# Wider input transfers for two batches, a last key chunk of 128, and a residual turned by DMA in an attention and wave-MLP kernel

## The chip, the cores and the metric

The kernel runs on one NeuronCore of one Trainium2 chip. The core has five engines that run side by side, each in its own order: TensorE (PE, matmuls; its weight loads are listed as PEld), VectorE (DVE), ScalarE (ACT), GpSimd (POOL) and SyncE (SP, which here only issues DMAs). Inputs and outputs lie in HBM; the engines work on SBUF, and matmuls write PSUM. The metric is device time in microseconds (us), less is better. The time before is 260.9 us, the median of 11 runs (260.03 to 262.04).

## What is computed

Two stages, cut from the reference to what matters:

```python
# q, k, v: (8 batches, 8 heads, 576 positions, 64)
q_d, k_d, v_d = mean over 4 neighbouring positions          # 144 positions
out_up    = repeat(softmax(q_d k_d^T / 8) v_d, 4)           # pooled attention
out_local = softmax(where(|i - j| < 4, q k^T / 8, -1e9)) v  # banded attention
x = (out_up + out_local) as (8, 576, 512)                   # heads side by side
theta = x @ w_theta
y = w_tok_r @ (x * cos(theta)) + w_tok_i @ (x * sin(theta)) # over positions
u = x + y
out = u + relu(u @ w_ch)                                    # float32
```

## The kernel before

**Stages.** For each batch, steps named by one letter each are done: L loads q, k, v into float32 staging tiles (`st`, eight buffers); C casts them to bf16 (`q_tm`, `k_tm`, `v_w`); A turns q and k so that head dimensions lie on partitions (`qT`, `kT`, pairs of heads stacked on 128 partitions) and makes the pooled `qdT`, `kdP` and `vd`; S makes scores and their exponentials (`pd` pooled, `pm` banded, five chunks of keys) and masks the band; N makes the pooled output (`xd`, `xdT`), V the banded output (`tmp`), T turns it and adds both (`xT`); H makes theta and cosine and sine (`cs`), M and Z the products (`z`, nine blocks of 128 rows: real and imaginary for 576 positions); X mixes over positions with the turned weights (`psu` from `WT` and `z`, eight products of nine matmuls of 288 columns a batch) and adds `xT` (`uT`); U turns `uT` by a transposing DMA into `utm`; R multiplies by `w_ch` (`psr`); O adds the residual and stores. Lower-case l and c load and cast the weights, W turns the token weights (nine `WT` blocks), and D is a warm-up of six matmuls of 512 columns that computes nothing.

**Order.** The steps of all kinds are laid out by hand as strings of letters: `FIRST`, then `PERIOD` three times, then `LAST`. A letter means the next step of its kind. After each step `pin()` ties every instruction to the one before it on its engine, so the strings are the order on each engine and on SP's queue of DMA issues. All input DMAs and all but one store are issued by SP.

**Chunks.** Queries are cut at 0, 120, 240, 360, 480 (`QS`); the keys that a chunk of queries can see start at `KS` and are `KW` long: four chunks of 128 and a last one from 476 of 100. For the pooled v, 120 positions of each chunk are summed by the matrices `PU` (one for the first chunk, one for the others). The mask of a chunk is a pair of affine selects on POOL (lines 442 and 444), for batch 0 a product with a `band` matrix on DVE (line 435).

**Batches 0 and 1** (`WIDE`) load q and k in another form than the rest (line 92): partition p holds positions 6p to 6p+5 of a head, so 96 partitions are used and a contiguous run is 6 x 64 floats, 1.5 KB; a transfer holds heads 2hh and 2hh+1, and there are four for q and four for k. `wide_turn` (from line 299) then turns one pair of heads with six matmuls of 96 columns, copies the result (q on ACT, k on DVE, line 309) and sums groups of four on DVE (lines 316, 319, 322). Later batches load positions onto partitions with runs of one head, 256 B. Casts of batch 0 are split: q on DVE, k on ACT, v on POOL; all later ones are POOL's.

**Residual.** For batches in `DMA_U` (1 to 6) the residual of the first 512 positions is `utm`, turned by DMA (line 621, one issue for each of four blocks of 128 channels), and DVE does relu and sum in one instruction (line 673). For batches 0 and 7 PE turns it into PSUM (`psx`, line 642), ACT applies relu (line 662) and DVE adds (line 678). The last 64 positions are always done in the second way.

Of the kernel before, what the change touches and what calls it, by code (L numbers as in the profile page):

```python
# [15 lines left out]
P = 128  # L16
# [12 lines left out]
QC = [120, 120, 120, 120, 96]  # L29
KS = [0, 116, 236, 356, 476]  # L30
KW = [128, 128, 128, 128, 100]
QN = [128, 128, 128, 128, 96]
# [3 lines left out]
TR = 96  # L36
NTR = 6
TP = TR // 4
TW = TR + TP

# [7 lines left out]
def kernel(  # L48
# [34 lines left out]
    def stage(b, key):  # L83
        t = staged[b, key] = stg.tile([P, 1024], FP32, tag="st", name=f"st{b}_{key}")
        return t

    def load(b):

        if b < WIDE:
            for hh in range(4):  # L90
                for nm, src in zip("qk", (q, k)):
                    nc.sync.dma_start(
                        out=stage(b, f"{nm}{hh}")[0:TR, 0:2 * NTR * D].rearrange("p (h e) -> p h e", h=2),
                        in_=src[b, 2 * hh:2 * hh + 2].rearrange("h (p r) d -> p h (r d)", r=NTR),
                    )
                    yield
        else:
            for nm, src in zip("qk", (q, k)):
                for i in range(3):
                    t = stage(b, f"{nm}{i}")[0:TR].rearrange("p (c h d) -> p c h d", c=2, d=D)  # L100
                    for j in range(2):
                        c = 2 * i + j
                        nc.sync.dma_start(
                            out=t[:, j], in_=src[b, :, TR * c:TR * c + TR, :].rearrange("h p d -> p h d"),
                        )
                    yield
        for i in range(3):
            t = stage(b, f"v{i}").rearrange("p (c h d) -> p c h d", c=2, d=D)
            for c in range(2 * i, min(2 * i + 2, NCH)):
                nc.sync.dma_start(  # L110
                    out=t[0:KW[c], c % 2],
                    in_=v[b, :, KS[c]:KS[c] + KW[c], :].rearrange("h p d -> p h d"),
                )
            yield

    def cast(b):

        q_tm = work.tile([TR, NTR, H, D], BF16, tag="q_tm", bufs=1, name=f"q_tm{b}")
        k_tm = work.tile([TR, NTR, H, D], BF16, tag="k_tm", bufs=1, name=f"k_tm{b}")
        v_w = v_ws[b % 2]  # L120
        inputs[b] = (q_tm, k_tm, v_w)
        eng = CASTS.get(b, CASTS[None])
        if b < WIDE:
            for hh in range(4):
                for i, dst in enumerate((q_tm, k_tm)):
                    eng[i](out=dst[:, :, 2 * hh:2 * hh + 2, :].rearrange("p r h d -> p h r d"),
                           in_=staged.pop((b, f"{'qk'[i]}{hh}"))[0:TR, 0:2 * NTR * D].rearrange(
                               "p (h r d) -> p h r d", h=2, d=D))
                    yield
        else:  # L130
            for i, dst in enumerate((q_tm, k_tm)):
                for c in range(3):
                    eng[i](out=dst[:, 2 * c:2 * c + 2].rearrange("p c h d -> p (c h d)"),  # L133
                           in_=staged.pop((b, f"{'qk'[i]}{c}"))[0:TR])
                    yield
        for i in range(3):
            t = staged.pop((b, f"v{i}")).rearrange("p (c h d) -> p c h d", c=2, d=D)
            n, rows = (2, P) if i < 2 else (1, KW[4])
            eng[2](out=v_w[0:rows, 2 * i:2 * i + n, :, 0:D], in_=t[0:rows, 0:n])  # L139
            yield  # L140
# [46 lines left out]
    PU = []  # L187
    for lo in (0, 4):
        r = const.tile([P, KP], BF16, name=f"pu{lo}")
# [15 lines left out]
    band = []  # L205
    for off in (3, -1):
        r = const.tile([P, P], BF16, name=f"band{len(band)}")
# [20 lines left out]
    def weight_loads():  # L228

        def two(w, nm):  # L230
            for i in range(2):
                nc.sync.dma_start(out=stage("w", f"{nm}{i}").rearrange("p (c e) -> p c e", c=2),
                                  in_=w[256 * i:256 * i + 256, :].rearrange("(c p) e -> p c e", p=P))
                yield
# [11 lines left out]
    def weight_casts():  # L246

        for i in range(2):
            act(out=wth[:, 2 * i:2 * i + 2, :].rearrange("p c e -> p (c e)"), in_=staged.pop(("w", f"th{i}")))
            yield  # L250
# [6 lines left out]
        for i in range(2):  # L257
            gp(out=wch[:, 2 * i:2 * i + 2, :].rearrange("p c e -> p (c e)"), in_=staged.pop(("w", f"ch{i}")))
            yield
# [32 lines left out]
    def turns(b):  # L292
# [8 lines left out]
        def wide_turn(n, hh):  # L301
            tm, To = ((q_tm, qT), (k_tm, kT))[n]
            ps = w2(f"pstr{n}{hh}_{b}")
            for r in range(NTR):
                nc.tensor.matmul(
                    out=ps[:, r // 3, (r % 3) * TR:(r % 3) * TR + TR],
                    lhsT=tm[:, r, 2 * hh:2 * hh + 2, :], rhs=ip[:, 0:TR], start=True, stop=True,
                )
            (dve if n == 1 else act)(
                out=To[:, hh, :].rearrange("p (w k c) -> p w k c", k=2, c=3),  # L310
                in_=ps[:, :, 0:3 * TR].rearrange("p k (c w) -> p w k c", w=TR),
            )
# [12 lines left out]
        def turn(n, c):  # L325
            tm, To = ((q_tm, qT), (k_tm, kT))[n]
            ps = w1(f"pstr{n}{c}_{b}")[:, 0:4 * TW].rearrange("p (hh w) -> p hh w", w=TW)
            for hh in range(4):
                nc.tensor.matmul(  # L329
                    out=ps[:, hh, :], lhsT=tm[:, c, 2 * hh:2 * hh + 2, :], rhs=ip, start=True, stop=True,  # L330
                )
# [23 lines left out]
        for c in range(4):  # L355
            nc.tensor.matmul(out=psb[KP * c:KP * c + KP, 0:2 * D], lhsT=PU[1][0:KW[4], :],
                             rhs=v_w[0:KW[4], 4, c::4, 0:D], start=True, stop=True)
# [14 lines left out]
    def scores(b):  # L372
# [28 lines left out]
        for h in range(H):  # L401
            par, r = h % 2, KP * (h % 4)
            nc.tensor.matmul(
                out=ps[r:r + KP, h // 4, SD:2 * SD],
                lhsT=kdP[64 * par:64 * par + 64, h // 2, 4, :],
                rhs=qdT[64 * par:64 * par + 64, h // 2, :],
                start=True, stop=True,
            )
# [7 lines left out]
        for c in range(NCH):  # L416
# [17 lines left out]
            if b in DVE_BANDS and c % DVE_BANDS[b] == 0:  # L434
                nc.vector.tensor_tensor(
                    out=pv, in0=pv,
                    in1=band[min(c, 1)][0:kw, 0:qn].unsqueeze(1).to_broadcast([kw, 8, qn]),
                    op=ALU.mult,
# [13 lines left out]
    def pooled_out(b):  # L452
# [3 lines left out]
        for g in range(2):  # L456
            ps = w2(f"psnd{g}_{b}")
            pv = ps[:, :, 0:260].rearrange("p e (j w) -> p e j w", w=65)[0:QD]
            for h in range(H):
                nc.tensor.matmul(  # L460
                    out=pv[:, h // 4, h % 4, :],
                    lhsT=pd[:, h, QD * g:QD * g + QD], rhs=vd[:, 0, h, 0:65],
                    start=(h % 4 == 0), stop=False,
                )
# [24 lines left out]
    def outputs(b):  # L489

        v_w = inputs.pop(b)[2]
        for c in range(NCH):
# [3 lines left out]
            for par in range(2):  # L496
                for j in range(4):
                    nc.tensor.matmul(  # L498
                        out=pv[0:qn, par, j, :],
                        lhsT=pms[b][c][0:kw, 4 * par + j, 0:qn],  # L500
                        rhs=v_w[0:kw, c, 2 * j + par, 0:65],
                        start=(j == 0), stop=(j == 3),
                    )
            rl = work.tile([P, 2, 4], FP32, tag="rl", name=f"rl{c}_{b}")
            nc.vector.reciprocal(out=rl[0:cnt], in_=pv[0:cnt, :, :, 64])
            tmp = tmps[b, c] = work.tile([P, DM], BF16, tag="tmp", bufs=4, name=f"tmp{c}_{b}")
            nc.vector.tensor_tensor(  # L507
                out=tmp[0:cnt].rearrange("p (j e d) -> p e j d", e=2, j=4),
                in0=pv[0:cnt, :, :, 0:D],
                in1=rl[0:cnt].unsqueeze(3).to_broadcast([cnt, 2, 4, D]),  # L510
                op=ALU.mult,
# [105 lines left out]
    def residuals(b):  # L617

        u = u_tm[b] = moep.tile([P, 4, 4, P], BF16, tag="utm", bufs=1, name=f"utm_{b}")
        for dc in range(4):  # L620
            nc.sync.dma_start_transpose(out=u[:, dc], in_=uTs[b][:, dc, 0:512])
            yield
# [44 lines left out]
    def store(b):  # L667
# [19 lines left out]

    DMA_U = (1, 2, 3, 4, 5, 6)

# [5 lines left out]
    FIRST = (  # L695
        "LLLCCLCALLALLCCALACDLCLADACAlAlCSSSClCSLASlScDVlNCcNAlNlVcSDlLcccWcTCLTcVVLHTAZCLVCHTCWALWWWLLTLLCCA"
        "LCWZWAAHLLAHWHADLWCSLCCCMZCLLZASlZlLCXSXACANSAACXLCSLNAAAXNSSXVAccCAXTCALVAACVLXLSTTSSHLVVXLTLHCTZRO"
        "AHZZCLHVLROHRLLMCOCSZZCNRLROSLNALOA"
    )
    PERIOD = (  # L700
        "XSCSNTXCCAAXCUAAVAXUACVAXAVAAVXTSSTAXSTAUTHXULCNHZNCAHLZCVHHCZROLLSLMSZRLOZRORLOLROL"
    )
    PERIODS = 3
    LAST = (
        "ASXVAAAXAAVXACCNAVXAUTACCCSUTTXTASSCXAHXVZUNHCTHXCAUHZNHZSZLLLRCMOLARORSSCZLRSOOCCNAXAXACAVAAVXXAVTA"
        "XUSSTARVXSOSXASTTHVUXVTHUNHZUZHNZHRMOSSZRORZORVXSONXTVTXXTVHXVXUHTZXTZHZUUHXZHMURROZROOXXRORXOXXXXRO"
        "ROXRORORORO"
    )
# [60 lines left out]
```

## Time and profile before

One execution was recorded by the hardware profiler; it took 259.36 us, of which the profile spans 257.6.

| | us |
|---|---|
| median of 11 runs (lowest, highest) | 260.9 (260.03, 262.04) |
| the profiled execution | 259.36 |
| its span, first to last instruction | 257.6 |
| mix products, line 608, 576 matmuls, busy | 80.0 |
| theta, line 546, 128 matmuls, busy | 32.9 |
| products with w_ch, line 632, 128 matmuls, busy | 32.0 |
| POOL's band selects, lines 442 and 444, busy | 73.5 |
| POOL waiting for DMAs of v, k (both forms) and q | 10.2, 8.3 + 6.4, 2.2 |
| warm-ups, line 282, 30 matmuls, busy | 10.4 |

A page of the profile gives busy time of each engine, the span in 40 slices with tenths of busy time, groups of instructions by line with mean duration and what ended the idle time ahead of them, and the chain of work that ended last. A name such as `k_tm<-st_k` is a tile and what it is made from. Matmul ends are modelled: a busy PE is not PE at its peak.

### The profile page before, as it was taken

How to read it: one execution, taken by the hardware profiler on the slowest of the kernel's cores; microseconds unless marked ns; L12 is line 12 of the kernel's file. 1: busy time of each engine (PE TensorE's matmuls, PEld its weight loads, DVE VectorE, ACT ScalarE, POOL GpSimd, SP SyncE). 2: the span in 40 equal slices, each digit the busy share in tenths (PEclk: the TensorE clock that was granted, in tenths of full speed). 3: DMA queues.
4: the chain of work that ended last, by engine and by line, in shares of the span. 5: the costliest groups of instructions: out<-in, count | busy, mean ns of one | idle time of the engine just before them, and what ended most of it. 6: DMA issues, size and time to landing. Idle time of an engine off the chain costs nothing.

```text
span 257.6 us, 7472 instructions
## 1 busy us (share of the span) xinstructions
PE 239.7 (93%) x2960; PEld 168.3 (65%) x2960; DVE 187.5 (73%) x421; ACT 179.0 (69%) x336; POOL 154.6 (60%) x178
## 2 busy tenths in 40 slices
PE   1868869999999999999999999999999999999993
PEld 1434546678667876587657866686768675776762
DVE  4866869767768777768686868785768588876543
ACT  3449489987988779867895689767885887334022
POOL 4244356599997977596839965898079763600000
PEclk9986999999999999999999999999999999999998
DMA  7999999999998994999689987998399122311324
GB/s 188 249 249 319 274 253 193 217 236 240 206 233 214 243 163 95 202 235 260 84 193 223 280 117 158 198 269 191 74 248 222 34 53 87 100 41 43 149 71 150
DMA packets 120851, 46.73 MB, mean 181 GB/s; under 512 B 110448, under 2 KB 114544, under 8 KB 120816
## 3 DMA queue, kind: packets, MB, share of 16 engines
q1 hardware_dynamic: 120736, 46.18, 81.8%
q8 instruction: 23, 0.38, 0.7%
q14 instruction: 12, 0.10, 0.1%
q10 hardware_dynamic: 80, 0.07, 0.1%
HBM read 33.65 MB, written 9.44 MB: 167 GB/s over the span
## 4 chain that ended last, share of the span: by engine, by line
PE 81%; DMA 7%; ACT 4%; DVE 3%; POOL 2%; issue 1%; SPq 1%; DVEq 0%; POOLq 0%
PE psu L608 27%; PE psr L632 10%; PE psth L546 10%; PE pstr L329 6%; DMA w<-in_moe_w_tok_i_dram 5%; PE psS L421 4%; PE psloc L498 3%; PE xTps L528 3%; PE psxt L581 3%; PE wu L282 2%; DMA st_k<-in_k_dram 2%; PE psnd L460 2%; PE psr L650 2%; PE pstl L557 1%; PE psnd L466 1%; PE pszl L592 1%
## 5 line engine op out<-in xcount | busy, mean ns | idle before, releaser
L608 PE MATMUL psu<-WT,z 128*128 128x288 bf16 x576 | 80.0, 286 | 0.0
L608 PEld LDWEIGHTS <-z 128*128 128x128 bf16 x576 | 53.6, 98 | 15.3 <-issue 0.8
L442 POOL TENSOR_SCALAR_AFFINE_SELECT pm<-pm 128x1024 bf16<-128x1024 bf16 (+1 forms) x35 | 36.7, 1050 | 22.2 <-ACT pm L429 22.1
L612 DVE TENSOR_TENSOR uT<-psu,xT 128x288 bf16<-128x288 f32 x64 | 29.2, 456 | 24.1 <-PE psu L608 23.2
L429 ACT ACTIVATE pm<-psS 128x1024 bf16<-128x1024 f32 (+1 forms) x40 | 38.1, 986 | 10.3 <-PE psS L421 10.1
L444 POOL TENSOR_SCALAR_AFFINE_SELECT pm<-pm 128x1024 bf16<-128x1024 bf16 (+1 forms) x35 | 36.8, 1051 | 2.4
L546 PE MATMUL psth<-wth,xT 128*128 128x512 bf16 x128 | 32.9, 379 | 0.6 <-DVE xT L529 0.6
L632 PE MATMUL psr<-wch,uT 128*128 128x512 bf16 x128 | 32.0, 380 | 0.0
L551 ACT ACTIVATE cs<-psth,pihc 128x512 bf16<-128x512 f32 x32 | 22.1, 689 | 11.6 <-PE psth L546 7.9
L507 DVE TENSOR_TENSOR tmp<-psloc,rl 120x512 bf16<-120x512 f32 (+1 forms) x40 | 27.6, 690 | 1.4
L529 DVE TENSOR_TENSOR xT<-xTps,xdT 128x480 bf16<-128x480 bf16 (+1 forms) x40 | 25.0, 632 | 3.5 <-PE xTps L528 2.9
L139 POOL CAST v_w<-st_v 128x1024 bf16<-128x1024 f32 (+1 forms) x24 | 20.9, 899 | 10.2 <-DMA st_v<-in_v_dram 10.2
L582 DVE TENSOR_TENSOR z<-psxt,cs 128x1024 bf16<-128x1024 bf16 x32 | 21.7, 686 | 4.7 <-PE psxt L581 3.2
L133 POOL CAST k_tm<-st_k 96x1024 bf16<-96x1024 f32 x18 | 18.8, 1047 | 9.3 <-DMA st_k<-in_k_dram 8.3
L332 ACT CAST kT<-pstr 128x384 bf16<-128x384 f32 x36 | 18.0, 502 | 7.0 <-PE pstr L329 6.9
L662 ACT ACTIVATE rel<-psr 128x512 f32<-128x512 f32 (+1 forms) x16 | 7.9, 494 | 18.4 <-PE psr L650 15.0
L133 POOL CAST q_tm<-st_q 96x1024 bf16<-96x1024 f32 x18 | 18.4, 1037 | 2.2 <-DMA st_q<-in_q_dram 2.2
L332 ACT CAST qT<-pstr 128x384 bf16<-128x384 f32 x36 | 16.1, 483 | 4.9 <-PE pstr L329 4.7
L552 ACT ACTIVATE cs<-psth 128x512 bf16<-128x512 f32 x32 | 18.9, 591 | 0.0
L673 DVE SCALAR_TENSOR_TENSOR osb<-psr,utm 128x512 f32<-128x512 f32 x24 | 16.4, 688 | 2.4 <-PE psr L632 2.0
L632 PEld LDWEIGHTS <-uT 128*128 128x128 bf16 x128 | 11.1, 98 | 9.8
L498 PE MATMUL psloc<-v_w,pm 128*128 128x65 bf16 (+1 forms) x320 | 16.9, 196 | 0.1
(107 smaller groups left out, 433.0 us busy)
## 6 DMA issues: line engine op xcount, KB each, us to landing
st_v<-in_v_dram SPq DMA_DIRECT2D x32, 256.0 KB, 5.0
out_dram<-osb SPq DMA_DIRECT2D x32, 256.0 KB, 3.7
st_q<-in_q_dram SPq DMA_DIRECT2D x36, 192.0 KB, 4.7
st_k<-in_k_dram SPq DMA_DIRECT2D x36, 192.0 KB, 4.3
st_q<-in_q_dram SPq DMA_DIRECT2D x8, 288.0 KB, 5.9
st_k<-in_k_dram SPq DMA_DIRECT2D x8, 288.0 KB, 11.6
st_v<-in_v_dram SPq DMA_DIRECT2D x8, 200.0 KB
w<-in_moe_w_tok_r_dram SPq DMA_DIRECT2D x2, 576.0 KB
```

What stands on the lines that cost most here:

```text
L133: eng[i](out=dst[:, 2 * c:2 * c + 2].rearrange("p c h d -> p (c h d)"), in_=staged.pop((b, f"{'qk'[i]}{c}"))[0:TR])
L332: nc.scalar.copy(out=To[:, :, TR * c:TR * c + TR], in_=ps[:, :, 0:TR])
L429: nc.scalar.activation(out=pv, in_=ps[0:kw].rearrange("p e (j w) -> p (e j) w", w=P)[:, :, 0:qn], func=AF.Exp, scale=SCL,)
L442: nc.gpsimd.affine_select(out=pv, in_=pv, compare_op=ALU.is_ge, fill=0.0, base=off, pattern=[[0, 8], [-1, qn]], channel_multiplier=1)
L444: nc.gpsimd.affine_select(out=pv, in_=pv, compare_op=ALU.is_ge, fill=0.0, base=6 - off, pattern=[[0, 8], [1, qn]], channel_multiplier=-1)
L498: nc.tensor.matmul(out=pv[0:qn, par, j, :], lhsT=pms[b][c][0:kw, 4 * par + j, 0:qn], rhs=v_w[0:kw, c, 2 * j + par, 0:65], start=(j == 0), ...
L507: nc.vector.tensor_tensor(out=tmp[0:cnt].rearrange("p (j e d) -> p e j d", e=2, j=4), in0=pv[0:cnt, :, :, 0:D], in1=rl[0:cnt].unsqueeze(3) ...
L529: nc.vector.tensor_tensor(out=xT[:, :, QS[c]:QS[c] + cnt].rearrange("p e (m j) -> p e m j", j=4), in0=ps[:, :, 0:cnt].rearrange("p e (m j) ...
L546: nc.tensor.matmul(out=th, lhsT=xT[:, dc, P * c:P * c + P], rhs=wth[:, dc, :], start=(dc == 0), stop=(dc == 3),)
L608: nc.tensor.matmul(out=ps[:, 0:288], lhsT=z[:, j, P * dc:P * dc + P], rhs=WT[:, j, cols], start=(j == 0), stop=(j == 8),)
L612: nc.vector.tensor_tensor(out=uT[:, dc, cols], in0=ps[:, 0:288], in1=xT[:, dc, cols], op=ALU.add)
L632: nc.tensor.matmul(out=psr, lhsT=uT[:, dc, P * c:P * c + P], rhs=wch[:, dc, :], start=(dc == 0), stop=(dc == 3),)
```

## The change

q and k of batches 0 and 1 are read with nine positions to a partition: 64 partitions hold one head, two neighbouring heads fill 128, and a contiguous run is 9 x 64 floats, 2.3 KB. A staging tile takes two such transfers, heads (4g, 4g+1) and (4g+2, 4g+3), and is cast at once into a layout in which heads h and h+2 lie side by side on a partition. So a pair that is turned together is h and h+2; `place` gives pair and half of a head, and the pooled, banded and output steps ask it. Turning takes nine matmuls of 64 columns. The last key chunk starts at 448 and is 128 long, with a pooling matrix and a band matrix of its own. Batch 7 joins `DMA_U`; its last block of 128 channels is turned by four PE transposes and copied by ACT. All three order strings are new; the number of warm-ups stays five.

```diff
-KS = [0, 116, 236, 356, 476]
-KW = [128, 128, 128, 128, 100]
+KS = [0, 116, 236, 356, 448]
+KW = [128, 128, 128, 128, 128]
...
+WR = 9
+WB = 64
...
-            for hh in range(4):
+            for g in range(2):
                 for nm, src in zip("qk", (q, k)):
-                    nc.sync.dma_start(
-                        out=stage(b, f"{nm}{hh}")[0:TR, 0:2 * NTR * D].rearrange("p (h e) -> p h e", h=2),
-                        in_=src[b, 2 * hh:2 * hh + 2].rearrange("h (p r) d -> p h (r d)", r=NTR),
-                    )
+                    t = stage(b, f"{nm}{g}").rearrange("p (e r d) -> p e (r d)", e=2, d=D)
+                    for e in range(2):
+                        h = 4 * g + 2 * e
+                        nc.sync.dma_start(
+                            out=t[:, e], in_=src[b, h:h + 2].rearrange("h (p r) d -> (h p) (r d)", r=WR),
+                        )
                     yield
...
+    def place(b, h):
+
+        return (2 * (h // 4) + h % 2, h // 2 % 2) if b < WIDE else (h // 2, h % 2)
+
+    def wide(t, g):
+
+        return t.rearrange("p c h d -> p (c h d)")[:, 2 * WR * D * g:2 * WR * D * (g + 1)].rearrange(
+            "p (r e d) -> p r e d", e=2, d=D)
...
-            for hh in range(4):
+            for g in range(2):
                 for i, dst in enumerate((q_tm, k_tm)):
-                    eng[i](out=dst[:, :, 2 * hh:2 * hh + 2, :].rearrange("p r h d -> p h r d"),
-                           in_=staged.pop((b, f"{'qk'[i]}{hh}"))[0:TR, 0:2 * NTR * D].rearrange(
-                               "p (h r d) -> p h r d", h=2, d=D))
+                    eng[i](out=wide(dst, g).rearrange("p r e d -> p e r d"),
+                           in_=staged.pop((b, f"{'qk'[i]}{g}")).rearrange("p (e r d) -> p e r d", e=2, d=D))
                     yield
...
-    for lo in (0, 4):
+    for lo in (0, 4, 32):
...
-    for off in (3, -1):
+    for off in (3, -1, -29):
...
-            for r in range(NTR):
+            flat = ps.rearrange("p k n -> p (k n)")[:, 0:S]
+            for r in range(WR):
                 nc.tensor.matmul(
-                    out=ps[:, r // 3, (r % 3) * TR:(r % 3) * TR + TR],
-                    lhsT=tm[:, r, 2 * hh:2 * hh + 2, :], rhs=ip[:, 0:TR], start=True, stop=True,
+                    out=flat[:, WB * r:WB * r + WB], lhsT=wide(tm, hh // 2)[:, r, :, :],
+                    rhs=ident[:, WB * (hh % 2):WB * (hh % 2) + WB], start=True, stop=True,
                 )
...
-            nc.tensor.matmul(out=psb[KP * c:KP * c + KP, 0:2 * D], lhsT=PU[1][0:KW[4], :],
+            nc.tensor.matmul(out=psb[KP * c:KP * c + KP, 0:2 * D], lhsT=PU[2],
                              rhs=v_w[0:KW[4], 4, c::4, 0:D], start=True, stop=True)
...
-            nc.sync.dma_start_transpose(out=u[:, dc], in_=uTs[b][:, dc, 0:512])
+            if b < B - 1 or dc < 3:
+                nc.sync.dma_start_transpose(out=u[:, dc], in_=uTs[b][:, dc, 0:512])
+            else:
+                ps = w1(f"psut_{b}", BF16)[:, 0:512].rearrange("p (c t) -> p c t", t=P)
+                for c in range(4):
+                    nc.tensor.transpose(out=ps[:, c, :], in_=uTs[b][:, dc, P * c:P * c + P], identity=ident)
+                nc.scalar.copy(out=u[:, dc], in_=ps)
             yield
...
-    DMA_U = (1, 2, 3, 4, 5, 6)
+    DMA_U = (1, 2, 3, 4, 5, 6, 7)
...
     FIRST = (
-        "LLLCCLCALLALLCCALACDLCLADACAlAlCSSSClCSLASlScDVlNCcNAlNlVcSDlLcccWcTCLTcVVLHTAZCLVCHTCWALWWWLLTLLCCA"
-        "LCWZWAAHLLAHWHADLWCSLCCCMZCLLZASlZlLCXSXACANSAACXLCSLNAAAXNSSXVAccCAXTCALVAACVLXLSTTSSHLVVXLTLHCTZRO"
-        "AHZZCLHVLROHRLLMCOCSZZCNRLROSLNALOA"
+        "LCLALLCLAllALCCALAAAclCDASDSCSllSSClllALVSLcDccNcccLCcNDCVLVLNTVWWSWLTCTCWLLLACVWHTTACLACHZHAAHALHAD"
+        "WAASZMCZCLZSCWSLlWNZWNCAAACSXNVAAASXTALSLXVLALAXALTSVLCHCTCVXCCHlcVTAXCTcACHZLHCXHZASLSXLZZRLROCSMLR"
+        "OOLSRZOLCSCLLNROALA"
     )
     PERIOD = (
-        "XSCSNTXCCAAXCUAAVAXUACVAXAVAAVXTSSTAXSTAUTHXULCNHZNCAHLZCVHHCZROLLSLMSZRLOZRORLOLROL"
+        "CCANAXAASCSXCANXVAVAXVUAAXLAVASTXCATSSTUATVUHXXHZTHNCUZHRLCLCOHZSLSLMCZROZLRRLORLLOO"
     )
...
     LAST = (
-        "ASXVAAAXAAVXACCNAVXAUTACCCSUTTXTASSCXAHXVZUNHCTHXCAUHZNHZSZLLLRCMOLARORSSCZLRSOOCCNAXAXACAVAAVXXAVTA"
-        "XUSSTARVXSOSXASTTHVUXVTHUNHZUZHNZHRMOSSZRORZORVXSONXTVTXXTVHXVXUHTZXTZHZUUHXZHMURROZROOXXRORXOXXXXRO"
-        "ROXRORORORO"
+        "LAVCACAASXLAVAXAACVNAUAXSSNLXCVATCSTCAASVCUXAATSNAAXASNAUXSSNTTHVXVUZHTHZHTVLHRAOROMCAROALZHZCZSROVC"
+        "CAXTXSSUTAVXZSSTXHVHNNXZUHVNXHMRZSSOXZZXTVUXTUXRTHOVVXHRROOTXZTROHXZXZHUXXZHMURUUROZROXROOXXROXXUXXX"
+        "UURUORORRRROROOO"
     )
```

## The prediction

> **What bounds the kernel now.** First the page: how full each engine is, and where.
>
> ```profile
> span 257.6 us, 7472 instructions
> ...
> PE 239.7 (93%) x2960; PEld 168.3 (65%) x2960; DVE 187.5 (73%) x421; ACT 179.0 (69%) x336; POOL 154.6 (60%) x178
> ...
> PE   1868869999999999999999999999999999999993
> ...
> DMA  7999999999998994999689987998399122311324
> ```
>
> The span is 40 slices of 6.44 us. TensorE (PE) is full from slice 7 (about 40 us) to the end; only the first 40 us and the last slice have holes. So the order of the later work matters only if it makes a hole, and the time is: when PE becomes full, plus the matmul work left. I count that work in columns of the moving operand. Between the first mix products (psu, dc 0, first half) of batches 1 and 2, which the chain of waits starts at 81.77 and 109.03 us, lie 66,824 columns: 2,451 per us. Before batch 0's first mix product (49.13 us) stand 64,776. In all there are 557,504.
>
> The holes before 40 us are read from two more views. The windows (busy time with count for each engine, granted clock, DMA share, GB/s) show what the queue moves when only one kind of load is in it:
>
> ```profile
> 4.00:11.00 7.00, 4.61 (x30) 2.61 (x31) 5.69 (x18) 3.57 (x5) 3.50 (x12) 1.00 1.09 261
> 11.00:16.00 5.00, 4.36 (x38) 2.38 (x36) 3.42 (x8) 2.01 (x3) 1.04 (x1) 1.00 1.31 215
> 18.00:22.00 4.00, 3.62 (x51) 2.03 (x52) 1.50 (x4) 3.15 (x6) 0.62 (x1) 0.50 1.02 368
> 33.00:37.00 4.00, 1.79 (x24) 1.32 (x25) 2.12 (x4) 3.81 (x5) 2.20 (x3) 1.00 1.09 265
> ```
>
> Rows 1 and 4 are q and k of batches 0 and 1 (96 partitions, runs of 1.5 KB): 261 and 265 GB/s. Row 2 is v (runs of 256 B): 215. Row 3 is mostly theta and the token weights, 128 partitions, runs of 2 to 2.3 KB: 368. The DMA share is full throughout: the queue is the bottleneck of the inputs. The waits between 20 and 50 us (total, times, longest) say who suffers:
>
> ```profile
> POOL k_tm L126 <- DMA st_k<-in_k_dram: 6.4, 4, 5.6
> ...
> PE pstr L305 <- POOL k_tm L126: 2.3, 1, 2.3
> POOL v_w L139 <- DMA st_v<-in_v_dram: 2.3, 3, 1.0
> POOL q_tm L133 <- DMA st_q<-in_q_dram: 2.2, 2, 1.1
> ...
> ACT wtm L253 <- DMA w<-in_moe_w_tok_i_dram: 1.8, 2, 1.0
> ```
>
> Batch 1's k, the token weights, then batch 2's q arrive late. VectorE (DVE) bounds only batch 0's turns: busy from 4.67 to 18.24 us with some 2 us of gaps.
>
> **The change, part by part.**
>
> *Transfers of q, k.* 2 x 2.36 MB. At 263 GB/s 18.0 us, at the nearest row (368, same run length and partitions) 12.8: 2.6 us less queue per batch. The Trainium skill (SBUF — State Buffer, "Door 1: The DMA port swizzle") says that the rate follows the ports reached, and its table puts partitions 0-63 on the 8 even ports; so 96 partitions send two thirds of their bytes through half of the ports, and 128 should give 4/3 of 263, 350, an estimate: 2.25 us per batch. I take the row; below, nothing is gained if run length and partitions don't matter. SP's issues stay 8 per batch (0.45 us each).
>
> *Casts.* Per batch 8 of 96x768 become 4 of 128x1152. By elements per partition, DVE 4 x 0.53 becomes 2 x 0.80, ACT 4 x 0.83 becomes 2 x 1.25, POOL 8 x 0.83 becomes 4 x 1.24. But a first cast needs two transfers: q ends at 5.9 instead of 5.2. ACT now has the first qT copy ahead of its k cast, which therefore ends near 8.5 (6.05 before).
>
> *Turns.* 6 matmuls of 96 columns become 9 of 64: 576 either way, and L557 runs 16 of 64 columns in 0.47. Nothing. Copies and sums keep their 576 elements.
>
> *Last key chunk of 128.* The mask costs 880 ns at 100x768 against 1094 at 128x1024, a step of free size and not of partitions, so exp, masks and v casts stay. v grows by 8 x 57 KB, 2.1 us of queue over the run at 215 GB/s, only 0.5 of it before 50 us. The third pooling matrix and band cost POOL 1.5 us (two selects of 0.34, one of 0.21, two of 0.30), inside its 6.2 us wait before the first v, and DVE 0.2 of memsets ahead of the first q cast, inside the later landing.
>
> *Residual of batch 7.* 16 PE transposes (0.22 per four) become 4: -1,536 columns, 0.63 us of PE at 2,451. ACT loses four relus of 0.6 and gains a copy of 0.6; DVE's four sums keep 688 ns. SP gains three transposing DMAs (2.5 to land). The third follows the mix product two before the last (2.1 us before its end), so it lands about 1 us after that end; its first reader needs it at 2.2. Behind it SP only holds stores of batches 6 and 7. The PE transpose waits for a 0.46 us sum under psr4 and psx of batch 6 (1.1 us). If such a cover fails, up to 1 us of tail.
>
> *The new order, up to the first mix product.* DVE: with kT 0.79, kdP 0.73 and qdT 0.68 a step, k's cast at 8.5 and its turn 0.6 at cold clock, three qdT, four kT and kdP and one cast from 9.1 on come to 18.0. Two warm-ups (6 matmuls each) now stand inside: one ahead of k's last turn, one between psSd0 and psSd1. Their price:
>
> ```profile
> 8.83 2.76 PE L282 MATMUL wu<-warm,ident 128*128 128x512 bf16 x6
> ...
> 11.87 2.30 PE L282 MATMUL wu<-warm,ident 128*128 128x512 bf16 x6
> 14.01 0.42 PE L305 MATMUL pstr<-ip,k_tm 96*128 96x96 bf16 x6
> ```
>
> In the chain of waits the first takes 2.56 us, 427 ns a matmul, though the clock column still says 1.00; the one at 45.34 takes 1.30, full speed. The rule that speaks against the change is the skill's "TensorE: Matmul & The Clock Gate", Part 1: about 3.4 us of activity release the clock. Here it took from 9.04 to about 13.7. In the new order the first warm-up starts near 14.2, when k's second cast and the first gaps are over: by the rule PE is fast from 17.6 and the second warm-up costs 1.3, by the row from 18.9 and it costs 2.1. I take 1.7 and psSd1 at 19.6 (18.14 before): 1.5 us lost here.
>
> ACT from there: pm of chunk 0 starts at 20.6 (19.4 before). Up to the last WT copy it now also has batch 1's two pd, one table load, one pm and the vd copies (4.6 us more, less one wth cast moved forward), 28.5 to 29.3 in all: 49.5 without a gap. DVE from its first band product (21.6) to the last z needs 27 us: 48.9. Will inputs hold them up? Queue by bytes from 2.1 us: q, k to 8.5; v 1.31 MB at 215 to 14.6; theta and token weights 3.71 MB at 368 to 24.7, at the 294 measured over 17 to 33.5 to 27.2; q, k of batch 1 to 31.1 or 33.6 (last cast 40.7 before); v to 37 or 40 (46). PE now waits for the third cast of the imaginary token weights (wps1), behind which chunk 4's scores, further xTps and all of batch 1's turns are queued; it is ready at 29.5 to 30 (34.36 before), because ACT no longer waits for the load. If the load came at 33.5 as before, that would be 3.5 us of everything.
>
> So batch 0's first mix product can start at 49.9; I allow 0.5 for releases, 50.4. It has 70,344 columns before it. The old kernel is there at 49.13 + 5,568 / 2,451 = 51.4: **-1.0**.
>
> *From there to batch 1's first mix product*, the old kernel takes 32.64 us for 75,504 columns, 30.8 at rate: 1.8 lost, with POOL busy without a gap from 49.7 to 78 (masks, k_tm, v_w). POOL now has batch 2's q before its masks start at 48.7 (52.86 before), and five masks and two k casts end near 61, not 66.4. I take 1.0 of the 1.8: **-1.0**. After that PE is full in both; the period keeps its work, only shuffled: 0, between -0.5 and +1.5. Tail: **-0.6**. Sum -2.6 on the profiled execution's 259.36 (span 257.6): 256.8. That execution lies 1.5 below the median of the 11 runs and under their lowest, so on the median's scale 260.9 - 2.6 = **258.3**.
>
> **Rivals.**
> B, hidden transfer: the inputs come sooner, but the in-order start (8.5 for k, the warm-ups) and ACT's longer list make the first mix product start at 51.4, no gain, POOL's lead is eaten, and only the tail is left: 260.9 - 0.6 = 260.3. For it: DVE is almost gapless from 4.7 to 18 us. Against it: waits of 12.7 us in total for inputs (6.4 + 2.3 + 2.2 + 1.8). The same time comes if wide transfers run at 263.
> C, slower: the late, half-clock start of batch 0's scores is carried through. Cold warm-ups cost 2.6 each, psSd1 is at 20.6; then ACT with 29 us of work and 3 us of gaps (2.7 before) ends WT at 53.5, the first mix product starts 2.4 us after 51.4 and POOL's masks follow. 260.9 + 2.4 - 0.6 = 262.7. It decides from a start of 52.8 on (0.6 of tail and 0.8 of margin eaten). For it: every link is in order on its engine. Against it: DVE and ACT have idle time in the old trace just where loads were late.
>
> **Numbers.** Forecast case 0.68, B 0.17, C 0.15. A measurement here tells 0.3% (0.8 us) from no change. Of the forecast case 0.64 is beyond it; B straddles it: 0.06 faster, 0.08 same, 0.03 slower; C is slower. With 0.04 of the first as same: faster 0.70, same 0.12, slower 0.18. Low end: 2.0 at the first product, 1.8 recovered, 0.5 by the new period, 0.6 tail, 256.0; high end into C, 262.0.
>
> **What would show it.** Right: 350 GB/s or more in 3 to 8 us; batch 1's last k cast before 36; POOL waiting for k_tm under 2 us; first mix product at 49.5 to 51; warm-up 2 near 1.7; psSd1 near 19.6. Wrong: 265 GB/s in the wide loads (B), a first mix product after 52.8 (C), PE holes over 0.5 us in a period after 80 us, which nothing above prices.

## The result, and the profile after

The changed kernel takes 257.43 us, median of 12 runs (256.40 to 260.30), beside 260.88 for the kernel before in 47 runs. The ratio is 0.9873 (95% interval 0.9851 to 0.9895): 3.3 us less, between 2.7 and 3.9. The forecast was 258.3. The profiled execution took 257.23 us (span 255.5), 2.13 less than the profiled one of before.

The page: span, busy time of the engines, and the slices of PE and the queue.

```profile
span 255.5 us, 7542 instructions
...
PE 236.8 (93%) x2996; PEld 168.9 (66%) x2996; DVE 185.6 (73%) x421; ACT 176.0 (69%) x331; POOL 153.8 (60%) x179
...
PE   1497889899999999999999999999999999999993
...
DMA  6999989999999995997699979998965203152435
```

The first six slices of PE read 1, 4, 9, 7, 8, 8 now and 1, 8, 6, 8, 8, 6 before: batch 0's start is thinner, what follows is fuller. The windows (busy time with count, granted clock, DMA share, GB/s), the four stretches shown of before and one more:

```profile
4.00:11.00 7.00, 2.44 (x36) 2.01 (x36) 4.28 (x16) 3.09 (x4) 4.42 (x17) 1.00 1.09 316
11.00:16.00 5.00, 3.99 (x33) 2.40 (x34) 4.93 (x10) 2.71 (x4) 1.04 (x1) 1.00 1.12 300
18.00:22.00 4.00, 3.02 (x48) 1.42 (x46) 1.33 (x3) 2.84 (x5) 1.60 (x2) 1.00 1.01 333
28.00:32.00 4.00, 2.93 (x46) 2.02 (x44) 2.98 (x7) 3.67 (x6) 1.27 (x2) 1.00 1.06 387
33.00:37.00 4.00, 3.46 (x47) 2.28 (x47) 3.97 (x8) 3.90 (x7) 3.12 (x3) 1.00 0.83 173
```

q and k of batch 0 come at 316 GB/s instead of 261. By 28 to 32 us the queue is at batch 1's q and k, at 387; before, that was at 33 to 37 and 265. The clock column is 1.00 in the third row, where before had 0.50. The waits from 20 to 50 us (total, times, longest):

```profile
POOL v_w L152 <- DMA st_v<-in_v_dram: 2.6, 3, 1.2
...
ACT wtm L266 <- DMA w<-in_moe_w_tok_i_dram: 2.1, 2, 1.7
...
POOL k_tm L140 <- DMA st_k<-in_k_dram: 0.7, 2, 0.4
```

Waiting for batch 1's k fell from 6.4 us to 0.7, and PE's 2.3 behind it is gone. Waiting for the imaginary token weights did not fall (1.8 before).

**Where the gain sits.** VectorE adds each mix product to `xT` (line 629; 64 sums). The start of the first sum of batch 0, of batch 1, and of the last sum, in all profiled executions of this study (us), with the median of each kernel's runs. The last column is for batch 0's last chunk of keys: start and duration of VectorE's product of its exponentials with the band (line 449, in the old kernel 435).

| kernel | batch 0 | batch 1 | last | span | median | last band product |
|---|---|---|---|---|---|---|
| before | 50.50 | 82.92 | 249.72 | 257.6 | 260.9 | 29.50, 0.55 |
| before, once more | 53.55 | 85.92 | 252.72 | 260.6 | | 33.02, 1.00 |
| after | 51.63 | 81.29 | 246.21 | 255.5 | 257.4 | 32.27, 0.56 |
| runs of 256 B | 60.83 | 90.49 | 255.33 | 264.6 | 265.7 | 35.39, 1.01 |
| runs of 768 B | 53.08 | 82.74 | 247.57 | 256.9 | 258.7 | 33.10, 1.17 |
| old order, wide loads | 53.07 | 85.48 | 252.28 | 260.7 | 261.6 | 33.98, 1.10 |
| old residual | 50.46 | 80.12 | 244.96 | 255.2 | 258.4 | 31.10, 0.56 |
| old key chunk | 50.92 | 80.63 | 246.31 | 255.5 | 257.0 | 31.56, 0.56 |
| two warm-ups less | 52.13 | 81.79 | 246.62 | 255.9 | 257.8 | 32.17, 1.15 |
| no early warm-ups | 53.36 | 83.02 | 248.22 | 257.5 | 258.3 | 31.87, 1.55 |
| theta late | 52.92 | 82.58 | 247.75 | 257.0 | 257.4 | 31.02, 2.55 |
| theta late, two warm-ups less | 51.86 | 81.52 | 246.57 | 255.8 | 257.4 | 32.50, 0.56 |
| theta late, float32 operands | 51.72 | 81.38 | 246.37 | 255.6 | 257.7 | 30.20, 1.85 |
| float32 operands alone | 54.39 | 84.05 | 248.91 | 258.2 | 258.4 | 32.44, 1.94 |

At equal columns of matmul work, after leads before by 1.16 us at its first mix product (50.24 us; the old kernel has done as many columns at 51.4), by 2.0 at batch 1 and still by 2.0 at the first sums of batch 4, by 1.66 at batch 7, and by 2.1 at the end. The table says two things more. From batch 0 to batch 1 every kernel with the new order takes 29.66 to 29.71 us and every one with the old order 32.37 to 32.42, however late the inputs are. And nearly all that differs between executions lies ahead of the first sum: from it to the last one the new order takes 194.5 to 194.9 us (195.4 once).

The last column says where ahead of it. In six of the eleven traces with the new order the first sum starts 18.80 or 18.81 us after the end of that band product (after, 768 B, old residual, old key chunk, two warm-ups less, theta late with two warm-ups less), and in the changed kernel VectorE has no recorded wait between the two. In the other five more is lost behind it: 19.35 to 20.01 us, or 24.4 with runs of 256 B. So what sets the first sum is when this product starts and how long it takes. In the changed kernel the chain of work that ended last (start, duration) leads from the load of the imaginary token weights to the exponentials `pm` that this product needs:

```profile
18.54 10.10 DMA w<-in_moe_w_tok_i_dram
28.65 0.02 issue
28.67 1.15 ACT wtm L266
29.82 0.57 ACT wtm L268
30.39 1.07 ACT WT L287 x2
31.46 0.05 ACT pm L443
```

The exponentials end at 32.17, and the product starts at 32.27. Behind them the chain takes a load of v that lands at 37.60; VectorE is busy all that time, so the path over the product is as long.

### The profile page after: what moved, and what is told of

It is laid out like the page before. It is cut to its first block, busy times and chain, and to the rows that moved or that the text cites. A ratio compares the mean times of both kernels' runs of the same rounds, so it can differ in the third digit from the quotient of the medians.

```text
span 255.5 us, 7542 instructions
## 1 busy us (share of the span) xinstructions
PE 236.8 (93%) x2996; PEld 168.9 (66%) x2996; DVE 185.6 (73%) x421; ACT 176.0 (69%) x331; POOL 153.8 (60%) x179
## 4 chain that ended last, share of the span: by engine, by line
PE 81%; DMA 8%; DVE 4%; ACT 3%; SPq 2%; issue 1%; ACTq 0%; DVEq 0%
PE psu L625 28%; PE psr L655 11%; PE psth L563 10%; PE pstr L343 6%; DMA w<-in_moe_w_tok_i_dram 4%; PE psS L435 4%; PE psloc L514 4%; PE xTps L545 3%; PE psxt L598 3%; DMA st_v<-in_v_dram 2%; DMA st_k<-in_k_dram 2%; PE psr L673 2%; PE psnd L475 2%; PE pstl L574 1%; PE psnd L481 1%; DVE kT L323 1%
## 5 line engine op out<-in xcount | busy, mean ns | idle before, releaser
L546 DVE TENSOR_TENSOR xT<-xTps,xdT 128x480 bf16<-128x480 bf16 (+1 forms) x40 | 24.7, 631 | 2.4 <-PE xTps L545 2.0
L696 DVE SCALAR_TENSOR_TENSOR osb<-psr,utm 128x512 f32<-128x512 f32 x28 | 19.2, 690 | 6.5 <-PE psr L655 6.1
L685 ACT ACTIVATE rel<-psr 128x256 f32<-128x256 f32 (+1 forms) x12 | 5.5, 455 | 18.9 <-PE psr L673 18.7
```

What stands on the lines that cost most here:

```text
L546: nc.vector.tensor_tensor(out=xT[:, :, QS[c]:QS[c] + cnt].rearrange("p e (m j) -> p e m j", j=4), in0=ps[:, :, 0:cnt].rearrange("p e (m j) ...
```

## Experiments

**1. Shorter runs in the wide loads.** The staging tile is interleaved, so that the same bytes reach the same 128 partitions in pieces of 256 B; the cast reads them back in order.

```diff
-t = stage(b, f"{nm}{g}").rearrange("p (e r d) -> p e (r d)", e=2, d=D)
+t = stage(b, f"{nm}{g}").rearrange("p (r e d) -> p e r d", e=2, d=D)
```

> The changed kernel, only with the staging tile of the wide q and k transfers interleaved (position, head pair, dimension), so that the same 128 partitions get nine runs of 256 B instead of one of 2.3 KB; the cast reads it back in that order; all order strings as changed. Theory T (the gain comes from the faster transfer): these loads fall from about 340 to about 215 GB/s (the rate of v's 256 B runs), 3.7 us more queue per batch, some 7 us over two; batch 0's first k cast ends 2 us later, batch 1's last k cast near 43 instead of 36.6, first mix product at 54 to 57 instead of 50.2, time 261.5 to 265. Rival O (the new order carries the gain, transfers are hidden): rate falls the same way, but the first mix product stays before 51.5 and the time within 257.4 to 258.5.

265.66 us (ratio to before 1.0156, 1.0110 to 1.0202). The rate, by the same view:

```profile
2.00:5.00 3.00, 0.00 (x0) 0.00 (x0) 2.05 (x29) 0.09 (x1) 0.64 (x4) 1.00 0.98 205
5.00:8.00 3.00, 0.66 (x9) 0.50 (x9) 0.76 (x1) 0.40 (x1) 2.59 (x12) 1.00 1.30 216
```

205 and 216 GB/s where the changed kernel had 306 and 338: v's rate, with q and k's partitions. The first sum comes 9.2 us later; it and the time are above theory T's ranges: the token weights land 3 us late, but behind them PE's order has batch 1's turns and its pooled v, and the last k cast (43.1 instead of 35.4) and the last v cast (50.5 instead of 41.2) hold PE up again. Rival O falls: the new order depends on the loads.

**2. Runs of 768 B**, three to a partition.

> The changed kernel with the staging tile of the wide q and k transfers cut in three: each partition gets three runs of 768 B instead of one of 2.3 KB, on the same 128 partitions, same order strings. Theory P (partitions and ports set the rate, run length matters only at 256 B): about 320 GB/s between 2 and 8 us as with 2.3 KB (323 over that stretch), first mix product within 1 us of the changed kernel's, time 257 to 258.5. Theory R (run length sets the rate): about 265, the first mix product 3 to 5 us later, time 260 to 262.5.

258.67 us (0.9927, 0.9898 to 0.9957).

```profile
2.00:5.00 3.00, 0.00 (x0) 0.00 (x0) 2.05 (x29) 0.08 (x1) 0.64 (x4) 1.00 0.87 256
5.00:8.00 3.00, 0.66 (x9) 0.50 (x9) 1.35 (x1) 0.49 (x1) 2.52 (x12) 1.00 0.96 290
```

256 and 290, between the two theories: about as fast as the old loads (271 and 263 in these stretches) with half their run length, on 128 partitions instead of 96. In batch 1's stretch, 28 to 32 us, it is 320, where the old loads had 265 and the changed kernel 387. So run length counts, and partitions too unless a longer run is the slower one. The first sum comes 1.45 us later than the changed kernel's: 0.84 because the last band product starts later, 0.61 because it takes longer (experiment 7 shows why it can). VectorE's two q casts of batch 0, which read a more broken tile, take 1.35 instead of 0.70 and 0.75 us and are part of the 0.84. So at a rate nearer to the old one than to the new the new order still gains 1.9 us (1.1 to 2.7) on the kernel before, and the longer runs are worth some 1.2 to 1.4 us beside it, uncertain by 1, the slower casts included; only where the rate falls further, as in experiment 1, is batch 1 late and much is lost.

**3. The old order with the wide loads alone**: old chunk, old residual, old strings, from which every second L and C of q and k of batches 0 and 1 is dropped.

> The kernel before with the wide transfers alone: its own order strings, from which only the second of each two load and cast letters of q and k of batches 0 and 1 is dropped (a load now brings two pairs), old key chunk, old residual, old DMA_U. Theory T: loads at 340 GB/s or more, the 2.3 us that PE waited for batch 1's k and the 1.8 of ACT for the token weights go, time 258.3 to 259.5. Rival O (order): the old order has its own holes at the same places, 260.3 to 261.5, the same as before. Rival C (the first k cast waits for two transfers and nothing is filled in): over 261.5.

261.62 us (1.0028, 1.0006 to 1.0049): not faster, and by the mechanism of rival C. ScalarE's timeline (start, duration) of this kernel:

```profile
7.53 1.28 ACT L140 ACT_TABLE_LOAD   x1 [7.53 <-DMA st_k<-in_k_dram]
8.82 1.15 ACT L140 CAST k_tm<-st_k 128x1152 bf16<-128x1152 f32 x1
9.88 0.63 ACT L323 CAST qT<-pstr 128x576 bf16<-128x576 f32 x1
```

In the old order k's cast is ScalarE's first work. It now waits for two transfers; a table load of 1.28 us falls behind that wait (it was at 0.80 us in the kernel before), and the first qT copy, for which VectorE waits 5.2 us, behind both. The new order puts the qT copy first (6.31) and the k cast after it (7.03). Batch 1 came sooner (its last k cast at 35.1 instead of 40.7), but the first sum went from 50.50 to 53.07. Theory T and the order are no rivals: the wide loads bring nothing in the old order, and the new order loses with runs of 256 B, though at 768 B it keeps more than half of its gain.

**4. Old residual.** Batch 7 leaves `DMA_U`, the last four U of `LAST` go.

> The changed kernel with batch 7's residual as before: 16 transposes on PE, four relus on ACT, no transposing DMAs, and the last four U letters dropped. Theory T: 12 transposes of 128 columns more, 1,536 columns at 2,451 per us, 0.6 us: 257.8 to 258.5. Rival (the removed transposes were under DVE's sums at the tail): 257.2 to 257.7, no difference. Rival (the DMA route delays the last stores): under 257.0.

258.36 us (0.9893, 0.9842 to 0.9944), inside theory T's range; the interval is too wide to tell 0.6. The trace can: from the start of the last sum to VectorE's end it takes 6.55 us here and 5.91 after, 0.63 more, and to the span's end 0.99. Its first sum came 1.17 us earlier than after's though all instructions up to there are the same, and so did the last band product: ScalarE cast the two large pieces of the imaginary token weights at 25.2 and 27.4 instead of 27.2 and 28.7 us. The chain no longer goes through that load but through TensorE's warm-ups and VectorE. So that landing was on the path in the profiled execution of after, and cost some 1.2 us there.

**5. Old key chunk**: 476 and 100 again, two `PU`, two `band`.

> The changed kernel with the last key chunk from 476 of 100 again, with two pooling and two band matrices. Theory T: 0.46 MB less to read (2.1 us of queue over the run, most of it where the queue isn't the bound) and 1.5 us less of POOL ahead of its first cast, all under other work: 257.0 to 257.8. Rival (the first turn waits for POOL's pooling matrices, or the queue of the first 50 us is on the path): 256.3 to 256.9.

256.98 us (0.9841, 0.9790 to 0.9892), inside the changed kernel's scatter and on the border between the two ranges given. The chunk's price is not told apart from 0.

**6. Warm-ups.** First the two early ones taken out (`WARM` 3), then the first four (`WARM` 1).

> The changed kernel without the first two of its five warm-ups (the one ahead of k's last turn of batch 0 and the one between the two pooled scores). Theory T (they stand in the path of VectorE and ScalarE, but the imaginary token weights land later anyway): first band exponential 1.0 to 1.3 us earlier (18.8 to 19.1 instead of 20.1), the wait of ScalarE for the token weights longer by as much, first mix product unchanged within 0.3, time 256.9 to 257.9. Rival (the start of batch 0 is on the path): first mix product 1 us earlier, 256.2 to 256.6. Rival (the warm-ups pay for themselves by the clock): turns and scores stay at half clock to 25 us and a half-clock stretch shows in the granted clock, over 258.2.

> The changed kernel without its first four warm-ups, so that TensorE warms by its own work only. Theory T (matmuls before 30 us are short and hidden, clock matters little there): turns, scores and transposes at half clock until some 3 us after TensorE gets dense (about 30 us), first band exponential 1 us earlier, transposes of the token weights 0.3 us longer each, 257.2 to 258.2. Rival (the warm-ups pay): a start of mix products 1.5 us later or more, over 258.8. Rival (they only stand in the way): under 256.9.

257.77 (0.9888, 0.9848 to 0.9928) and 258.27 us (0.9888, 0.9838 to 0.9939): neither is told apart from the changed kernel. Without the two, the last kdP is done 8.8 us after the first kT copy instead of 9.7: 0.9 us that the warm-ups cost this chain. The first band exponential came at 19.84, not by 19.1: k landed 0.95 us later in this execution. And the 0.9 is given back: the third, now the first, runs cold in the middle of batch 0's outputs, and VectorE waits for the products behind it (timeline of PE, then of DVE).

```profile
23.68 2.10 PE L295 MATMUL wu<-warm,ident 128*128 128x512 bf16 x5 [0.33 <-issue]
```

```profile
26.32 0.20 DVE L487 RECIPROCAL rd<-psnd 72x8 f32<-72x8 f32 x1 [1.17 <-PE psnd L481]
```

The last band product then starts 0.10 us earlier than in the changed kernel and takes 1.15 instead of 0.56 us. Without all four, ten transposes of the token weights take 1.49 us instead of 0.98 where PE is warm, and that product takes 1.55. What the warm-ups are worth is so not told apart from 0 here; no run takes them out with that product undisturbed and theta in its place.

**7. Is it the token weights' landing?** Theta's weights are loaded behind both token weights, and cast by GpSimd.

```diff
-        yield from two(moe_w_theta, "th")
         for ri, w in enumerate(w_tok):
...
+        yield from two(moe_w_theta, "th")
         yield from two(moe_w_ch, "ch")
```

> The changed kernel with the loads of theta's weights moved behind both token weights in the queue, and their two casts moved from ScalarE to GpSimd behind the token casts; nothing left out. Theory T (after the change the landing of the imaginary token weights sets the first mix product): they land 1.05 MB sooner, some 3 us; ScalarE's wait of 1.7 us for them goes and its cast at 24.4 too; VectorE's gap of 1.1 us at 31 us goes, and VectorE is then what bounds: first mix product 1.0 to 1.3 us earlier than 50.2, time 256.1 to 256.7. Rival (VectorE's chain bounds already, and the wait is only beside it): 257.2 to 257.8. Rival (theta arrives too late for GpSimd and then for batch 1's casts): over 258.

> Both together: theta late and no first two warm-ups. Theory T: with the token weights off the path the earlier start of batch 0 (1.0 to 1.3 us) counts as well: first mix product 1.8 to 2.4 us earlier than 50.2, 255.0 to 255.8. Rival (batch 1's inputs take over as the bound): no better than theta late alone, 256.1 to 256.7.

257.44 (0.9880, 0.9832 to 0.9929) and 257.38 us (0.9875, 0.9829 to 0.9922). The wait for the token weights went, as theory T said (ScalarE casts them at 24.2, without a wait), and the last band product of the first kernel starts 1.25 us earlier, at 31.02. Yet nothing was gained: the first rival has the time, and the second kernel is no better than the first. In the first of the two the timeline of all engines shows what came instead, in the lines of VectorE and GpSimd:

```profile
29.84 1.14 POOL L140 CAST q_tm<-st_q 128x1152 bf16<-128x1152 f32 x1
...
30.93 1.14 POOL L140 CAST k_tm<-st_k 128x1152 bf16<-128x1152 f32 x1
31.02 2.55 DVE L449 TENSOR_TENSOR pm<-pm,band 128x768 bf16<-128x768 bf16 x1
32.02 1.14 POOL L140 CAST q_tm<-st_q 128x1152 bf16<-128x1152 f32 x1
```

The product of the last chunk with its band takes 0.56 us in the changed kernel. Here it began 0.09 us after a cast of GpSimd and ended 0.4 us after the last of them: it waited through two casts and did not get in between. That took 2.0 us, and 0.55 more was lost behind it. The Trainium skill (SBUF — State Buffer, "SBUF: two separate sides") has VectorE and GpSimd share one pair of ports under an exclusive lock, which a VectorE instruction with two SBUF inputs needs against a GpSimd one that reads SBUF; the loser waits. By that rule VectorE's reads of PSUM beside these casts should not be held up, and they are not (`tmp`, 0.69 us throughout).

The six times of this kernel fall in two groups, 256.2 to 256.9 and 258.0 to 258.9 us, and the profiled execution (258.72) is of the second. That the first group is where the product goes ahead of the casts is likely but not shown. The second kernel was not held up by a cast; its warm-up ran cold, as in experiment 6, and the chain goes through it (timeline of all engines):

```profile
23.90 2.21 PE L295 MATMUL wu<-warm,ident 128*128 128x512 bf16 x5 [0.33 <-issue]
...
26.65 0.20 DVE L487 RECIPROCAL rd<-psnd 72x8 f32<-72x8 f32 x1 [1.28 <-PE psnd L481]
...
32.50 0.56 DVE L449 TENSOR_TENSOR pm<-pm,band 128x768 bf16<-128x768 bf16 x1
```

**8. Does a float32 operand avoid the lock?** The third band and the tile `csl` become float32, with theta late and without.

```diff
-r = const.tile([P, P], BF16, name=f"band{len(band)}")
+r = const.tile([P, P], FP32 if off == -29 else BF16, name=f"band{len(band)}")
```

> Theta late as before, and VectorE's two products that read SBUF only made float32 in one operand (the third band matrix and the tile of the last cosines and sines), which makes each slower by itself (0.48 to some 0.85 us, 0.42 to some 0.55). Theory K (in the kernel with theta late VectorE's 128x768 product took 2.55 us instead of 0.5 because it waited for the end of GpSimd's casts, three back to back, and the product of the last 64 positions takes 1.18 instead of 0.42 in all these kernels for the same reason): with a float32 operand neither waits; the two take under 1.0 and under 0.7 us; first mix product 1.7 to 2.4 us earlier than with theta late alone (52.9 to 50.5 to 51.2 at its sum), time 255.6 to 256.6. Rival (the 2.55 us came from half-clock TensorE or from the wait for the exponential): the product still ends near 33.5, time 257.2 to 257.8.

> The changed kernel with these two float32 operands alone, theta loaded where the change has it. Theory K: the product of the last 64 positions falls from 1.18 to under 0.7 us and VectorE's last z comes 0.5 us earlier, but the token weights land as before and ScalarE's last WT copy (49.55) then sets the start alone: first mix product 0 to 0.5 us earlier, 257.0 to 257.5. Rival (the two waits are all there is to gain, theta's place doesn't matter): as good as the two together, 255.6 to 256.6.

257.66 (0.9867, 0.9820 to 0.9913) and 258.38 us (0.9902, 0.9861 to 0.9943). The first has the time of the rival, the second is above both of its ranges. Theory K had the cause right and the cure wrong. The product still waits (first kernel, timeline of all engines):

```profile
30.11 1.14 POOL L140 CAST k_tm<-st_k 128x1152 bf16<-128x1152 f32 x1
30.20 1.85 DVE L449 TENSOR_TENSOR pm<-pm,band 128x768 bf16<-128x768 bf16 x1
31.56 1.50 POOL L140 CAST q_tm<-st_q 128x1152 bf16<-128x1152 f32 x1 [0.32 <-DMA st_q<-in_q_dram]
```

Two inputs in SBUF are enough, as the rule says, with one of them float32 too; when the cast ended at 31.25, the product needed 0.8 us. The small product of the last 64 positions went from 1.18 to 1.44 us. In the second kernel the two meet within 0.02 us, and in the changed kernel within 0.04, the other way round:

```profile
32.42 1.14 POOL L140 CAST k_tm<-st_k 128x1152 bf16<-128x1152 f32 x1 [0.30 <-PE wps L282]
32.44 1.94 DVE L449 TENSOR_TENSOR pm<-pm,band 128x768 bf16<-128x768 bf16 x1 [1.01 <-ACT pm L443]
```

```profile
32.27 0.56 DVE L449 TENSOR_TENSOR pm<-pm,band 128x768 bf16<-128x768 bf16 x1 [1.11 <-ACT pm L443]
32.31 1.52 POOL L140 CAST k_tm<-st_k 128x1152 bf16<-128x1152 f32 x1 [0.31 <-DMA st_k<-in_k_dram]
```

After wins by 0.04 us and the cast takes 1.52 instead of 1.15; the other loses by 0.02, and its first sum comes 2.8 us later. 1.4 of that is the product (some 0.25 of it the float32 operand), 0.2 its later start, and 1.2 is lost behind it. PE stands still for 1.73 us in it; the granted clock is then 0.58 from 34 to 38 us.

**9. The kernel before, once more.**

> The kernel before, unchanged, profiled once more. The two profiled executions of before and after differ by 2.1 us, the medians of all their runs by 3.4. Theory S (nearly all of that scatter lies ahead of the first mix product, in the landing of the inputs and in the half-clock stretch near 20 us): the spacing from the first to the last sum of u is 199.2 us again within 0.3, the first sum itself is off 50.5 by as much as the time is off 259.4, and later where the mean granted clock is lower than 0.983. Rival (scatter lies in the periods): the first sum is at 50.5 within 0.3 and the spacing differs.

262.35 us, 2.99 more than the first profiled execution; the first sum 3.05 later; the spacing 199.17 instead of 199.22; the mean granted clock 0.972 instead of 0.983. Theory S holds. The place of the 3 us, in this execution and then in the first:

```profile
23.28 4.26 DVE L435 TENSOR_TENSOR pm<-pm,band 128x1024 bf16<-128x1024 bf16 x2 [0.82 <-ACT pm L429]
23.79 1.02 POOL L126 CAST q_tm<-st_q 96x768 bf16<-96x768 f32 x1 [0.20 <-DMA st_q<-in_q_dram]
...
24.76 2.23 POOL L253 CAST wtm<-w 128x1152 bf16<-128x1152 f32 x2
```

```profile
22.95 1.61 DVE L435 TENSOR_TENSOR pm<-pm,band 128x1024 bf16<-128x1024 bf16 x2 [0.82 <-ACT pm L429]
23.90 1.34 POOL L126 CAST q_tm<-st_q 96x768 bf16<-96x768 f32 x1 [0.64 <-DVE pm L435]
```

The second of the two band products alone (timeline of VectorE from 24.15 and from 23.82 us), again in this execution and then in the first:

```profile
24.20 3.34 DVE L435 TENSOR_TENSOR pm<-pm,band 128x1024 bf16<-128x1024 bf16 x1
```

```profile
23.87 0.69 DVE L435 TENSOR_TENSOR pm<-pm,band 128x1024 bf16<-128x1024 bf16 x1
```

It lost to the q cast and to both token casts behind it; in the first execution it came 0.03 us before the cast. PE was idle for 2.9 us meanwhile, and its granted clock averaged 0.56 from 27 to 34 us, against 1.00.

## Why the prediction was right, and where not

**The number** was 0.9 too high; two errors partly cancel. The sum of steps was -2.6, the two profiled executions differ by -2.1, so the sum is 0.4 too good. And the step to the median's scale failed: "that execution lies 1.5 below the median" was added for both kernels, as if any execution lay as far below. It was a lucky one of before (experiment 9); after's lies 0.2 below its own median. That alone is worth 1.3; that the whole is nearer than this part is luck. The lost race of experiment 9 explains little of it. Its execution has a granted clock of 0.972. Of the 58 runs of the kernel before beside the experiments 16 have a clock below 0.98 (median 261.8 us), and without them the median falls from 260.6 to 260.2: if the low clock marks the lost race, it is worth 0.4 in the median. The rest of the 1.5, and how often after loses its own race, stays open.

**Transfers:** forecast 350 or more; batch 0 got 306 to 338 (340 from 3 to 8 us, so this sign was missed), batch 1 387. The row (368) was right where the queue was already full of bytes, too high at the start.

**Start of batch 0:** k's cast ended at 8.18 (8.5 said), the warm-ups took 2.75 and 1.71 (1.7 taken between rule and row), the second pooled score product psSd1 came at 19.03 (19.6), as this timeline of PE shows:

```profile
13.76 2.75 PE L295 MATMUL wu<-warm,ident 128*128 128x512 bf16 x6
16.30 0.69 PE L319 MATMUL pstr<-ident,k_tm 128*128 128x64 bf16 x9
16.92 0.54 PE L397 MATMUL psSd<-qdT,kdP 64*128 64x144 bf16 x6
17.39 1.71 PE L295 MATMUL wu<-warm,ident 128*128 128x512 bf16 x6
19.03 0.24 PE L397 MATMUL psSd<-qdT,kdP 64*128 64x144 bf16 x2
```

**First mix product:** 50.24 (50.4), the last WT copy ended at 49.55 (49.5), the last k cast of batch 1 began at 35.4 (before 36 said, 40.7 in the old kernel). -1.16 for -1.0. Two reasons under it were not right. The sum of the queue's bytes had the token weights landed by 24.7 to 27.2 us and ScalarE free of waiting for them; the last piece landed at 29.4, ScalarE waited 2.1 us (1.8 before), and the chain goes through this load. And the gain was read as inputs that come sooner. Experiment 3 shows that sooner inputs bring nothing in the old order, where the later first cast takes their gain back, experiment 2 that at a rate nearer to the old one 1.9 of the 3.3 us stay. So what the sooner inputs are worth is no term of its own: nothing in the old order; in the new one 1.2 to 1.4 us between runs of 768 B and 2.3 KB, and 8.2 between 256 B and 2.3 KB.

**To batch 1's first mix product:** -0.85 for -1.0. GpSimd's lead fits: its masks of batch 1 begin 1.6 us before the first mix product, 3.7 after it in the old kernel; and in this stretch the chain of the old kernel goes through two k casts and a mask of GpSimd (58.25 to 62.49 us), that of the changed one through none. No run changes the lead alone. And the lead is the order's: the spacing is 29.66 us even where all inputs are late, and 32.41 with wide loads in the old order.

**Period** 0 (0 said), with no hole of PE over 0.5 us after 80 us. **Last string:** 0.35 us is lost between batches 4 and 7, which nothing priced; its place was not found. **Tail:** -0.45 for -0.6; the residual's own part is 0.63 to VectorE's end (0.63 said), by experiment 4.

**Rivals:** B wanted a first mix product at 51.4 and only the tail as gain; the lead of 1.16 and 2.0 us speaks against it, and experiment 1 shows that the transfers are not hidden in the new order. C would have begun with a first mix product after 52.8. Its mechanism did not show; the lost race for the port would have brought it about (a first sum at 54.39, so a first mix product near 53.0), and the prediction did not have that race, though the trace of before shows both instructions and the section cited in experiment 7 names the lock.

## What to carry to other kernels

A wider transfer delays the first consumer while it speeds up the last: here it paid only with an order in which other work stands ahead of that first consumer. When the time of a kernel scatters by more than the change is worth, find the place of the scatter first, with two traces of the same kernel, before a sum is moved from one execution to the median. Beside a VectorE instruction with two SBUF inputs, look for what GpSimd does just then: back-to-back casts can hold it for their whole length.

## What the runs showed of the hardware

- A band product of 0.56 us became 2.55, and the second of a pair some 2.65 longer, behind two or three back-to-back casts on GpSimd; 0.02 to 0.04 us decide who goes first. In no version tried is it ruled out.
- Idle gaps of PE of 1.7 to 2.9 us (experiments 7, 8 and 9) were followed by 3 to 7 us at about half the granted clock; one of 2.3 us at 33 us of the kernel before was not (1.00 from 34 to 42 us). The Trainium skill (TensorE: Matmul & The Clock Gate, Part 1) puts the fall after an idle window of about 3.4 us; here shorter gaps among thin work were enough in three executions.
- On 128 partitions the queue moved 205 to 216 GB/s in runs of 256 B, 256 to 320 in 768 B, 306 to 387 in 2.3 KB; on 96 partitions 261 to 271 in 1.5 KB.
